# Chunk 5's gates by seven products, one of the sums on a PSUM bank that ScalarE fills, and a new order of the steps

## The chip, the cores and the metric

The kernel runs on one core of one Trainium2 chip. The metric is the device time of one execution in microseconds. A program's time is the median of its runs; the three runs of the kernel before lie between 249.38 and 249.58 us.

## The reference

Eight batches of 576 positions with 8 heads of 64 go through a linear attention, and the 4608 resulting rows of 512 go through a multiplicative feed-forward block:

```
phi(x) = where(x > 0, x, exp(x) - 1) + 1
kv  = sum over s of phi(k)[s] v[s]          z = sum over s of phi(k)[s]
x   = (phi(q) kv) / (phi(q) z + 1e-6)       per batch and head, then heads side by side
out = (((x @ w1) * (x @ w2)) @ w3) @ w_out  x: 4608 x 512, w1 and w2: 512 x 1024,
                                            w3: 1024 x 1024, w_out: 1024 x 512
```

Inputs and output are float32; the kernel's matmuls take bfloat16 and sum in float32.

## The kernel before

The product wf = w3 @ w_out is formed once, so each row of x needs two matrix products, the gates a = x w1 and b = x w2 with their elementwise product ab, and then out = ab wf. The rows are handled in 9 chunks of 512. Chunk c below 8 holds 512 of the 576 positions of batch c; chunk 8 holds the eight remainders of 64.

The program is a list of named steps, the string `ORDER`, carried out from left to right. `step` turns each name into a few instructions. The list alone sets in which order the instructions stand on each engine; the engines then run freely, each its own queue in order, and wait for one another by semaphores. The DMAs queue in the same way on SP and on POOL, and a DMA that waits holds back all that stand behind it on its queue. A `+` behind a step picks another engine for it: DVE in place of ScalarE for a copy, POOL in place of SP for a load. The steps that matter here:

- `L`, `M`, `N` load k, q and v of a batch in halves (512 KB each) into `ld` tiles, `R` the remainder of 64 positions (64 KB pieces, two for v, four for q and k).
- `x`, `y`, `z` (`X`, `Y`, `Z` for q) make phi of a half by ScalarE's exp (L179) and DVE's max and min (L184, L209); `v` casts v.
- `K` forms kv in a PSUM tile (L245), `T` transposes phi(q) by a DMA on SP into `qt` (L269), `A` multiplies the two and divides (L310, L326). `D` transposes the result `xn` by a DMA on SP into `xt` (L351), the moving operand of the gates; `D1.1`, `D3.1`, `D5.1`, `D7.1` do it for chunk 8 into `xtr`.
- `Fc.f` forms 128 columns of both gates of chunk c directly: eight matmuls with 512 moving columns into two banks `a_ps` and `b_ps` (L362), a ScalarE copy of one (L367), a DVE product with the other into `ab` (L368).
- `Gc.q.i` is used for chunks 6, 7 and 8 in place of `F`. It is Strassen's scheme with seven products for a 2 x 2 split of the weights' columns and the rows: product i of column pair q (columns q and q + 4) takes four matmuls with 256 moving columns (L422). It needs sums of weight blocks (steps `e`, kept in `ld` tiles named `spare`) and of xt blocks (steps `d`, L407). The products are summed in PSUM where they can be, in a bank `gu` (of the pool that the output also uses) and in banks `gt` of the pool `mm_ps`, which has four; where a bank is needed in two sums, ScalarE copies it into a half of a ring of `spare` tiles (L450) and DVE adds the copy to another bank (L454). Steps `m` then multiply the two gates, both in SBUF (L465), into `ab`; product 7 ends in a ScalarE copy of half a bank (L458) and a DVE product (L459).
- `Oc.m` is the output product of 128 rows of ab with wf: eight matmuls with 512 columns (L536), and a copy (L538). `S` and `H` store.

In the seven-product form a column pair has four quarters of ab to fill. Before, the quarter of products 1 and 2 is made as the others are: product 1 goes into `gu` and is copied to SBUF, product 2 goes into a bank of its own, DVE adds the two, DVE multiplies.

Of the kernel before, what the change touches and what calls it, by code (L numbers as in the profile page):

```python
# [20 lines left out]
def kernel(  # L21
# [388 lines left out]
    def g_product(t, c, q, a, m, first):  # L410

        for w in range(2):
            for k in range(2):
# [8 lines left out]
                nc.tensor.matmul(t[:, w], l, r, start=(first and w == 0 and k == 0), stop=(k == 1),  # L422
                                 skip_group_check=True)

    ring = []

    def fsm(name):
        if not spare.get("ring"):
            spare["ring"] = True
            for n in range(6):  # L430
                t = from_ld(("f", n), [P, 2, 2, HN], F32)
                ring.extend((t[:, 0], t[:, 1]))
        return ring.pop(0)

    def g_unit(c, q, i):
# [12 lines left out]
        if i in (1, 3, 4):  # L448
            s = st["s", i] = fsm("gs")
            nc.scalar.copy(out=s, in_=t)  # L450
        elif i in (2, 5, 6):
            s = st["c", i] = fsm("gc")
            o = st["s", {2: 1, 5: 4, 6: 3}[i]]
            nc.vector.tensor_tensor(out=s, in0=o, in1=t, op=ALU.add)  # L454
            ring.append(o)
        else:
            s = fsm("ga")
            nc.scalar.copy(out=s[:, 0], in_=t[:, 0])  # L458
            nc.vector.tensor_mul(out=abs_[c][:, q + 4, 0:HN], in0=s[:, 0], in1=t[:, 1])  # L459
            ring.append(s)  # L460

    def g_mul(c, q, i, alt):
        s = cs_[c, q]["c", i]
# [1 line left out]
        (nc.gpsimd if alt else nc.vector).tensor_mul(  # L465
            out=abs_[c][:, f, r * HN:(r + 1) * HN], in0=s[:, 0], in1=s[:, 1])
# [119 lines left out]
    A1.4 x2.1 F1.7 F1.6 x2.2 L2.0 y2.1 y2.2 Y2.0 x3.2 R3.1+ X2.0 O0.3 N2.1 x2.0 z2.1 N2.0 y2.0 z2.2  # L586
    Z2.0 F1.0 M3.0 R5.0+ y3.2 T2.0 v2.1 L3.0 Y3.1 R2.1+ F1.5 N3.1 v2.0+ z2.0 L3.1 Z3.1 v2.2+ O0.2
    F1.2 F1.1 Y3.0 y5.2 z3.2 K2 F1.4 A2.2 X3.0 F1.3 A2.3 x3.0 O0.1 Z3.0 A2.0 x3.1 N3.0 y3.0 O0.0
    v3.1 S0.1 A2.1 y3.1 R5.1+ z3.0 z3.1 v3.0 v3.2 O1.1+ O1.0 T3.0 D2.0 S0.0 L4.0 K3 R4.1+ R4.0+ O1.3
    A3.0 O1.2 A3.2 L4.1 v4.2+ F2.6 A3.3 F2.3 N4.1 y4.0 F2.1 M4.0 x4.0 A3.1 x4.1 F2.0 M4.1 y4.2 v5.2+  # L590
    x4.2 F2.7 Y4.0 D3.0 F2.4 z4.0 F2.2 X4.1 Y4.1 S1.0 F2.5 v4.1 Z4.1 N4.0 M5.0 X4.0 Z4.0 A3.4 z4.2
    y4.1 O2.3 F3.7 z4.1 M5.1 v4.0 A2.4 Y5.0 F3.6 L5.0 T4.0 M6.1 R6.0+ x5.2 Y5.1 X5.0 F3.1 N5.1 Z5.0
    S1.1 O2.2+ K4 F3.2 M6.0 x6.2 X5.1 A4.2 Z5.1 F3.4 z5.2 F3.5 y5.0 A4.1 F3.0 L5.1 F3.3 N5.0 y5.1
    X6.1 y6.2 O2.1 A4.3 R6.1+ N6.0 S2.1 x5.1 N6.1 v5.0+ T5.0 O2.0 x5.0 v5.1+ A4.0 R7.0+ z5.1 D4.0
# [5 lines left out]
    d6.0 v7.1 A6.4 e1.3 O5.1 O5.0 G6.1.1 G6.1.2 d6.1 G6.0.1 K7 d6.2 d6.3 G6.0.2 G6.0.3 m6.1.2 G6.0.4  # L600
    m6.0.2 S5.0 A7.3 G6.1.3 G6.0.5 G6.1.4 G6.1.5 m6.0.5 G6.2.4 G6.0.6 G6.0.7 G6.1.7 A7.0 G6.1.6
    G6.2.1 S4.0 G6.3.1 D5.1 G6.2.2 G6.2.3 G6.3.2 G6.3.3 m6.1.6 G6.2.5 G6.3.4 m6.2.2 G6.3.5 G6.2.6
    G6.2.7 A7.4 D7.1 G6.3.7 G6.3.6 O5.2 m6.3.5 A7.2 d8.0 O5.3 d8.2 G8.0.1 G8.0.4 m6.2.6 d8.1 m6.0.6
    d8.3 A7.1 G8.1.1 m6.3.6 G8.0.3 G8.0.2 G8.1.3 m6.2.5 G8.1.4 G8.0.5 G8.1.5 G8.3.4 G8.1.6 m8.0.2
    G8.0.7 G8.1.7 G8.2.4 m6.1.5 D7.0 G8.1.2 m8.0.5 d7.0 G8.2.1 S5.1 G8.3.1 G8.0.6 G8.2.3 m8.0.6
    G8.2.6 G8.3.3 G8.2.5 m6.3.2 G7.0.4 G8.3.5 G7.1.4 m8.1.2 G8.2.7 d7.1 G8.2.2 G8.3.7 d7.2 m8.1.5
    G8.3.6 O6.0 m8.3.5 m8.1.6 d7.3 O6.3 m8.2.5 O6.2+ m8.3.6 m8.2.6 O6.1 G7.0.1 m8.2.2 G8.3.2 G7.1.1
    m8.3.2 G7.0.3 S6.0 G7.0.6 G7.1.3 G7.0.5 G7.0.2 G7.1.5 G7.3.4 m7.1.5 G7.0.7 G7.2.4 m7.0.6 G7.1.7
    G7.1.6 m7.0.2 G7.2.1 G7.2.2 G7.3.1 S6.1 m7.2.2 G7.2.3 G7.2.6 G7.3.3 G7.2.5 G7.3.6 G7.3.5 G7.2.7
    G7.3.2 G7.1.2 G7.3.7 m7.3.2 m7.3.6 m7.1.2 O8.2 m7.3.5 O8.3 m7.0.5 O7.0 m7.2.6 O7.1 H8.2 m7.2.5  # L610
# [119 lines left out]
```

## Time and profile before

| | before |
|---|---|
| median of three runs | 249.55 us (249.38 to 249.58) |
| span of the profiled execution, first to last instruction | 248.0 us |
| own time of the profiled execution | not listed; its span stands 1.5 us below the median |
| TensorE (PE) busy | 230.9 us, 93% |
| VectorE (DVE) busy | 187.4 us, 76% |
| ScalarE (ACT) busy | 131.9 us, 53% |
| GpSimd (POOL) busy | 49.4 us, 20% |
| granted TensorE clock, mean | 0.991 |

The page divides the span into busy time by engine, and its groups by line give the mean duration of one instruction. PEld is the load of a matmul's stationary operand, which runs beside matmuls. Matmuls are pipelined: a group's mean of 379 ns is the time of one from its start to its modelled end, while the next one starts sooner, so the pace is read from the chain of waits, where runs of matmuls on one line are merged.

### The profile page before, as it was taken

To read this page: it belongs to the slowest core of one execution; us is meant where nothing else is said; L and a number is where in the kernel's file an instruction comes from. 1 tells how busy PE (TensorE), PEld (TensorE's weight loads), DVE (VectorE), ACT (ScalarE), POOL (GpSimd) and SP (SyncE) were. 2 spreads that over 40 slices of the span, in tenths; PEclk is the share of its full clock that TensorE was granted. 3 is DMA by queue.
4 is the path that set the end of the run, shared out by engine and by line. 5 is a ranking of instruction groups with operands and counts; after the bars stand their busy time and mean duration, and the time that the engine had idled before them with its cause. 6 is when DMAs were issued, how large, how long until landed. Compare 5 with 4: busy or idle time off the path is not lost.

```text
span 248.0 us, 4281 instructions
## 1 busy us (share of the span) xinstructions
PE 230.9 (93%) x1548; PEld 133.6 (54%) x1548; DVE 187.4 (76%) x434; ACT 131.9 (53%) x213; POOL 49.4 (20%) x79
## 2 busy tenths in 40 slices
PE   0699868999999999999999999999999999999994
PEld 0445455654454554345445544545488688578542
DVE  3227769777898847788768799988899999779810
ACT  2206667658756725675563383536466377245321
POOL 8546368665014050500000000000000000000000
...
GB/s 159 193 202 310 295 211 211 194 259 288 287 219 329 236 234 273 217 304 282 288 362 268 284 270 221 295 37 174 169 193 0 22 65 107 3 169 1 44 152 145
DMA packets 64021, 49.43 MB, mean 199 GB/s; under 512 B 32480, under 2 KB 58848, under 8 KB 64000
## 3 DMA queue, kind: packets, MB, share of 16 engines
...
q8 instruction: 12, 0.20, 0.3%
q10 hardware_dynamic: 144, 0.13, 0.2%
...
## 4 chain that ended last, share of the span: by engine, by line
PE 67%; DMA 21%; ACT 3%; DVE 3%; SPq 2%; issue 2%; POOL 0%; ACTq 0%; DVEq 0%; POOLq 0%
PE o_ps L536 21%; PE a_ps L362 12%; PE b_ps L362 12%; DMA q<-in_q_dram 10%; PE gu L422 9%; DMA w3b<-in_moe_w_dram 7%; PE gt L422 6%; DMA k<-in_k_dram 4%; PE nd L310 3%; PE kvp L245 2%; SPq L104 1%; ACT e L179 1%; PE o_ps L561 1%; PE kvp L249 1%; DVE qj L209 1%
## 5 line engine op out<-in xcount | busy, mean ns | idle before, releaser
L536 PE MATMUL o_ps<-wf_sb,ab 128*128 128x512 bf16 x280 | 64.2, 379 | 0.0
L362 PEld LDWEIGHTS <-w_sb 128*128 128x128 bf16 x384 | 36.5, 98 | 40.6 <-issue 0.8
L362 PE MATMUL a_ps<-xt,w_sb 128*128 128x512 bf16 x192 | 50.3, 379 | 0.5 <-ACT a_sb L367 0.5
L362 PE MATMUL b_ps<-xt,w_sb 128*128 128x512 bf16 x192 | 50.3, 379 | 0.0
L536 PEld LDWEIGHTS <-ab 128*128 128x128 bf16 x280 | 26.8, 98 | 29.3
L368 DVE TENSOR_TENSOR ab<-a_sb,b_ps 128x512 bf16<-128x512 f32 x48 | 32.5, 683 | 11.5 <-PE b_ps L362 5.9
L538 ACT COPY o_sb<-o_ps 128x512 f32<-128x512 f32 x30 | 17.4, 585 | 42.8 <-PE o_ps L536 28.8
L367 ACT COPY a_sb<-a_ps 128x512 f32<-128x512 f32 x48 | 27.7, 585 | 22.2 <-PE a_ps L362 21.8
L326 DVE TENSOR_TENSOR xn<-nd,r 128x512 bf16<-128x512 f32 x30 | 20.7, 691 | 1.0
L422 PEld LDWEIGHTS <-spare 128*128 128x128 bf16 x192 | 18.7, 98 | 2.2
L179 ACT ACTIVATE e<-q 128x1024 bf16<-128x1024 f32 x16 | 16.8, 1057 | 5.7 <-DMA q<-in_q_dram 5.0
L310 PE MATMUL nd<-kv,qt 128*128 128x130 bf16 (+1 forms) x160 | 16.6, 228 | 2.9 <-ACT kv L254 1.8
L179 ACT ACTIVATE e<-k 128x1024 bf16<-128x1024 f32 x16 | 16.8, 1056 | 3.2 <-DMA k<-in_k_dram 3.1
L310 PEld LDWEIGHTS <-qt 128*128 128x128 bf16 (+1 forms) x160 | 11.8, 103 | 12.2 <-issue 3.5
L454 DVE TENSOR_TENSOR spare<-spare,gt 128x512 f32<-128x512 f32 x24 | 16.1, 680 | 1.8 <-PE gt L422 0.9
L154 PE MATMUL wf_ps<-wt_sb,w3t 128*128 128x512 bf16 x64 | 16.5, 403 | 0.6 <-DMA wt_sb<-in_moe_w_out_dram 0.6
L450 ACT COPY spare<-gu 128x512 f32<-128x512 f32 x24 | 13.6, 587 | 3.9 <-PE gu L422 3.7
L422 PEld LDWEIGHTS <-w_sb 128*128 128x128 bf16 x144 | 14.0, 98 | 2.7 <-issue 0.3
L465 DVE TENSOR_TENSOR ab<-spare 128x256 bf16<-128x256 f32 x36 | 14.1, 417 | 0.1
L114 POOL DMA_DIRECT2D qk32r<-in_q_dram x14 | 9.0, 644 | 23.3 <-ACT a_sb L367 10.7
L209 DVE TENSOR_TENSOR qj<-e,y 128x512 bf16<-128x512 bf16 x32 | 12.1, 418 | 2.0 <-ACT e L179 1.8
L422 PE MATMUL gu<-spare 128*128 128x256 bf16 x96 | 13.4, 272 | 0.0
...
## 6 DMA issues: line engine op xcount, KB each, us to landing
out_dram<-o_sb SPq DMA_DIRECT2D x15, 512.0 KB, 3.9
q<-in_q_dram SPq DMA_DIRECT2D x13, 512.0 KB, 8.1
k<-in_k_dram SPq DMA_DIRECT2D x12, 512.0 KB, 7.0
v<-in_v_dram SPq DMA_DIRECT2D x12, 512.0 KB, 9.0
...
k<-in_k_dram POOLq DMA_DIRECT2D x4, 512.0 KB, 9.1
...
q<-in_q_dram POOLq DMA_DIRECT2D x3, 512.0 KB, 12.6
```

Of the source, the lines that this page charges most:

```text
L154: nc.tensor.matmul(wfs[i], w3ts[i][:, kc, :], wo_sb[:, kc, :], start=(kc == 0), stop=(kc == FC - 1))
L179: nc.scalar.activation(out=e, in_=x, func=AF.Exp)
L209: nc.vector.tensor_tensor(out=p[0][:, 2 * g + c].rearrange("p j u d -> p u j d"), in0=e[:, c], in1=y[:, c], op=ALU.min)
L310: nc.tensor.matmul(nds[g][rows, i * 2 * E1:(i + 1) * 2 * E1], w, kvs[b % 2][:, i, g].rearrange("p u e -> p (u e)"), start=True, stop=True)
L326: nc.vector.tensor_tensor(out=dst.rearrange("p (g h) e -> p g h e", g=2), in0=v4[:, :, :, 0:D], in1=r[rows].unsqueeze(3).to_broadcast([n, ...
L362: nc.tensor.matmul(ps, w[:, kc, f * P:(f + 1) * P], xt_of(c)[:, :, kc, :], start=(kc == 0), stop=(kc == KC - 1))
L367: nc.scalar.copy(out=a_sb, in_=a_ps)
L368: nc.vector.tensor_mul(out=abs_[c][:, f, :], in0=a_sb, in1=b_ps)
L422: nc.tensor.matmul(t[:, w], l, r, start=(first and w == 0 and k == 0), stop=(k == 1), skip_group_check=True)
L454: nc.vector.tensor_tensor(out=s, in0=o, in1=t, op=ALU.add)
L536: nc.tensor.matmul(o_ps, ab[:, f, m * P:(m + 1) * P], wf_sb[:, f, :], start=(f == 0), stop=(f == FC - 1))
L538: copy_of(alt)(out=rows_of(c, m // 2)[:, m % 2], in_=o_ps)
```

## The change

Chunk 5's gates are formed by the seven products too, so that `G` and `m` steps stand in the place of its eight `F` steps. For all four chunks in this form, the quarter of products 1 and 2 is made in another way: ScalarE copies product 1 from its bank `gu` into a bank `gt` instead of into SBUF, product 2 is accumulated onto that bank, and the quarter ends as that of product 7 does, with a ScalarE copy of half the bank and a DVE product of it with the other half. Four `m` steps with i = 2 per chunk and the DVE add of product 2 fall away. The weight sums of w1 now live in `wt_sb`, which held w_out for the prelude, not in `ld` tiles; the ring has 4 tiles in place of 6, and the small operands of products 2 and 7 lie in tiles of the pool `sm`. Of the list of steps the first 165 are as before; the rest is in another order, and some steps have another `+` (eight remainder DMAs move from POOL to SP).

```
     def ws_make(w, i, alt):
         t, s = (w1_sb, w2_sb)[w], wss[w]
-        s[i] = from_ld(("w", w, i // 2), [P, 2, 2, NQ * P], BF16)[:, i % 2]
+        if w == 0:
+            s[i] = wt_sb[:, i].rearrange("p a n -> p (a n)").rearrange("p (k n) -> p k n", k=2)
+        else:
+            s[i] = from_ld(("w", w, i // 2), [P, 2, 2, NQ * P], BF16)[:, i % 2]
...
+    NR = 4
...
-            for n in range(6):
+            for n in range(NR):
...
-        a, m, name, first = ((), ((0, 0, 0), (0, 0, 0), "u", True), ((0, 0, 1), (0, 1, 0), "t", True),
+        a, m, name, first = ((), ((0, 0, 0), (0, 0, 0), "u", True), ((0, 0, 1), (0, 1, 0), "t", False),
...
-        if i in (1, 3, 4):
+        if i == 1:
+            st["t"] = mm_ps.tile([P, 2, HN], F32, tag="mm", name="gt")
+            nc.scalar.copy(out=st["t"], in_=t)
+        elif i in (3, 4):
             s = st["s", i] = fsm("gs")
             nc.scalar.copy(out=s, in_=t)
-        elif i in (2, 5, 6):
+        elif i in (5, 6):
             s = st["c", i] = fsm("gc")
-            o = st["s", {2: 1, 5: 4, 6: 3}[i]]
+            o = st["s", {5: 4, 6: 3}[i]]
             nc.vector.tensor_tensor(out=s, in0=o, in1=t, op=ALU.add)
             ring.append(o)
         else:
-            s = fsm("ga")
-            nc.scalar.copy(out=s[:, 0], in_=t[:, 0])
-            nc.vector.tensor_mul(out=abs_[c][:, q + 4, 0:HN], in0=s[:, 0], in1=t[:, 1])
-            ring.append(s)
+            s = sm.tile([P, NCH], F32, tag="f", name="a_sb", bufs=4)[:, 0:HN]
+            nc.scalar.copy(out=s, in_=t[:, 0])
+            nc.vector.tensor_mul(out=abs_[c][:, q if i == 2 else q + 4, 0:HN], in0=s, in1=t[:, 1])
...
-        f, r = {2: (q, 0), 5: (q + 4, 1), 6: (q, 1)}[i]
+        f, r = {5: (q + 4, 1), 6: (q, 1)}[i]
...
     ORDER, a line of chunk 5 before and one after:
-    F4.1 S3.0 F4.4 D5.0 A5.4 y6.0 z6.0 F4.3 M7.1 F5.7 x7.2 y7.0 Y7.0 z7.2 L7.1 N7.0 K6+ z7.0 F5.6
+    N6.0 v6.0 D5.0 d5.2 d5.0 d5.1 N6.1 G5.0.1 R6.1 Z6.0 G5.1.1 F4.0 d5.3 G5.1.3 A4.4 G5.1.4 G5.0.3
```

On ScalarE's queue, at the start of chunk 7's gates, which both kernels form last: `o_ps` rows are the end of the output steps ahead of it, `gu` and `gt` are the banks of the products, `spare` is the ring in SBUF. Before:

```order
L538 COPY o_sb<-o_ps 128x512 x3
L450 COPY spare<-gu 128x512 x4
L450 COPY spare<-gt_2820 128x512
L458 COPY spare<-gu 128x256
L450 COPY spare<-gt_2833 128x512
L458 COPY spare<-gu 128x256
```

And now:

```order
L544 COPY o_sb<-o_ps 128x512 x3
L454 COPY gt<-gu 128x512
L457 COPY spare<-gt_2880 128x512
L454 COPY gt<-gu 128x512
L457 COPY spare<-gu 128x512 x2
L457 COPY spare<-gt_2915 128x512
L465 COPY a_sb<-gt 128x256
L465 COPY a_sb<-gu 128x256
```

The copy of product 1 goes into a bank now, and a second copy of half a bank (`a_sb<-gt`) has come in beside that of product 7.

On SP's queue, from the transpose of chunk 5's rows (`xt<-xn`) to the transpose of batch 6's phi(q) (`qt<-qj`). Before:

```order
L351 DMA_TRANSPOSE xt<-xn 128x16x128
L104 DMA q_1969<-in_q_dram 128x4x256
L104 DMA k_1993<-in_k_dram 128x4x256
L104 DMA v_1995<-in_v_dram 128x4x256
L546 DMA out_dram<-o_sb 128x1024
L269 DMA_TRANSPOSE qt<-qj 128x18x128 x2
```

And now:

```order
L351 DMA_TRANSPOSE xt<-xn 128x16x128
L104 DMA v_1937<-in_v_dram 128x4x256
L114 DMA v32r<-in_v_dram 64x4x64 x2
L104 DMA q_2017<-in_q_dram 128x4x256
L114 DMA qk32r<-in_q_dram 64x4x64 x2
L114 DMA qk32r<-in_k_dram 64x4x64 x2
L269 DMA_TRANSPOSE qt<-qj 128x18x128
```

Four DMAs stood between the two transposes, and eight stand there now, six of them the remainders that POOL issued before.

More of the change, by code (lines that the diff above doesn't have):

```diff
@@ L585 @@
     M2.1 M3.1 A1.3 F0.3 P1.3 X2.1 R2.0+ A1.0 L2.1 h0 h1 Y2.1 P1.0 M2.0 h2 h3 Z2.1 i0 i1 X3.1 R3.0+
[L586 to L594, printed above, removed]
@@ L600 @@
[L600 to L610, printed above, removed]
@@ L611 @@
-    H8.3 O8.0 m7.1.6 S7.0 O8.1+ S8.0 O7.2 H7.2 Q7.3
+    A1.4 x2.1 F1.7 F1.6 x2.2 N2.0 L2.0 M3.0 R3.1+ y2.2 O0.1 z2.2 R2.1+ v2.2+ Y2.0 Y3.1 X2.0 Z2.0
+    F1.1 N2.1 Z3.1 y2.0 F1.0 x2.0 z2.0 y2.1 z2.1 O0.3 L3.0 v2.0 v2.1 T2.0 y3.2 F1.3 x3.2 Y3.0 F1.4
+    L3.1 X3.0 Z3.0 K2 O0.0 y3.0 z3.2 x3.1 A2.2 F1.2 y3.1 N3.1 v3.1 A2.0 e0.2 x3.0 F1.5 N3.0 v3.0
+    S0.0 O0.2 A2.3 O1.3 z3.0 v3.2 A2.1 L4.1 x4.1 T3.0 R6.0+ R5.0+ z3.1 D2.0 S0.1 O1.2+ K3 O1.0 e1.2
+    A3.3 e1.0 L4.0 O1.1 A3.1 F2.6 A3.2 M4.0 F2.4 F2.1 y4.1 A3.0 F2.0 e1.1 F2.2 A3.4 S1.1 D3.0 R4.0+
@@ new lines @@
+    x4.2 y4.2 z4.2 X4.0 M5.1 M4.1 F2.5 z4.1 y4.0 x5.2 F2.7 S1.0 y5.2 Y4.0 z5.2 F2.3 x4.0 Z4.0 F3.4
+    F3.3 Y5.1 N4.1 z4.0 M5.0 Y4.1 R4.1+ v4.2 R5.1+ O2.0+ X4.1 Z4.1 N4.0 A2.4 F3.0 N5.1 v4.0+ F3.2
+    X5.0 v4.1+ T4.0 e0.0 Y5.0 F3.1 X5.1 Z5.1 v5.1 Z5.0 O2.1 K4 O2.2 A4.1 O2.3 L5.1 y5.1 A4.0 L5.0
+    y5.0 M6.1 y6.2 F3.5 x5.1 z5.1 S2.0 A4.2 Y6.1 X6.1 N5.0 F3.7 F3.6 x5.0 z5.0 S2.1 T5.0 A4.3 D4.0
+    v5.0 Z6.1 v5.2+ e0.1 O3.3 O3.0 K5 O3.1 e1.3 A5.3 M6.0 O3.2 e0.3 A5.0 D3.1 F4.5 A5.1 Y6.0 x6.2
+    z6.2 F4.2 F4.6 S3.0 A5.2 X6.0 L6.1 y6.1 x6.1 z6.1 F4.7 F4.3 A5.4 L6.0 x6.0 F4.4 y6.0 z6.0 F4.1
@@ new lines @@
+    A6.4 G6.0.3 G6.0.4 G6.1.5 G6.1.2 G6.0.5 m5.2.6 m6.0.5 K7 S5.0 G6.0.7 G6.0.6 G6.1.6 G6.1.7 G6.2.1
+    T7.0 A7.1 G6.2.4 G6.0.2 G6.2.3 G6.2.6 G6.3.1 G6.2.5 A7.4 G6.2.2 G6.3.3 G6.2.7 D7.1 G6.3.2 m5.0.5
+    G6.3.4 G6.3.5 A7.3 O5.2+ G6.3.7 G6.3.6 D1.1 d8.0 d8.1 m6.1.6 m6.2.5 m6.1.5 d8.2 A7.2 G8.0.1
+    m6.2.6 O5.3 G8.0.4 G8.0.3 m6.3.6 G8.1.1 G8.3.4 G8.0.6 d8.3 G8.0.5 G8.1.3 G8.0.2 G8.1.4 G8.1.5
+    G8.0.7 S5.1 G8.1.6 G8.1.2 G8.1.7 G8.2.1 G8.2.4 m8.0.6 m8.0.5 A7.0 G8.3.1 m8.1.6 G8.2.3 G8.2.6
+    G8.3.3 G8.2.5 G8.2.2 G8.3.5 G8.3.2 G8.2.7 G8.3.6 G8.3.7 S4.0 O8.0+ O8.1+ m6.0.6 D7.0 d7.0 O6.0
@@ L612 @@
+    S8.0 d7.1 m6.3.5 O6.3+ O6.2 O6.1 d7.2 G7.0.1 d7.3 G7.0.4 G7.1.1 m8.2.6 G7.0.3 G7.0.6 m8.1.5
+    G7.1.3 G7.0.5 G7.1.4 G7.1.5 G7.0.2 G7.0.7 G7.2.4 m8.3.6 m7.0.5 G7.1.7 G7.1.2 m7.1.5 G7.2.1
+    G7.1.6 m7.1.6 G7.3.1 G7.2.3 G7.2.6 G7.3.3 G7.2.5 m7.2.5 S6.1 G7.3.2 G7.3.4 G7.3.5 G7.2.7 G7.2.2
+    G7.3.6 G7.3.7 S6.0 O7.0+ m7.3.5 O7.1 S7.0 m8.3.5 m7.3.6 m8.2.5 O8.2 H8.2 O8.3 H8.3 m7.0.6 m7.2.6
+    O7.2 H7.2 Q7.3
     """
```

9 lines of the change are left out of this document (5 added, 4 removed).

## The prediction

> **What bounds the kernel now.** First the page's head, the busy time by stage and the granted clock; in the rows by stage the columns are PE, PEld, DVE, ACT and POOL busy, then the clock, the DMA engines' share and GB/s.
>
> ```profile
> span 248.0 us, 4281 instructions
> PE 230.9 (93%) x1548; PEld 133.6 (54%) x1548; DVE 187.4 (76%) x434; ACT 131.9 (53%) x213; POOL 49.4 (20%) x79
> ...
> 45.00:125.00 80.00, 79.27 (x493) 40.17 (x491) 63.70 (x147) 49.06 (x77) 22.08 (x36) 1.00 1.12 265
> 125.00:175.00 50.00, 49.53 (x289) 24.68 (x288) 43.07 (x98) 26.07 (x39) 0.00 (x0) 1.00 0.93 232
> 175.00:243.00 68.00, 67.99 (x511) 47.97 (x510) 54.50 (x124) 33.69 (x65) 0.00 (x0) 1.00 0.29 85
> ```
>
> From 45 us to 243 us TensorE is busy for 196.8 of 198 us at the full clock. The 165 steps that stay as they are end in this stretch (at about 62 to 64 us), so what is reordered is all work of a saturated TensorE. The time of the reordered part is the sum of its matmuls plus TensorE's waits; another engine matters only where TensorE waits for it. DVE is second, with 54.5 of 68 us in the last stage.
>
> A busy row could hide a slow pace, so next the chain of waits (start, length, what), where merged runs give the true pace, and TensorE's waits (total us, times, longest):
>
> ```profile
> 60.36 0.86 PE b_ps L362 x4
> ...
> 91.59 12.85 DMA q<-in_q_dram
> ...
> 118.44 9.40 DMA k<-in_k_dram
> ...
> 185.55 0.44 PE gt L422 x4
> ```
>
> ```profile
> PE nd L310 <- DVE xn L326: 0.8, 2, 0.5
> PE a_ps L362 <- ACT a_sb L367: 0.5, 1, 0.5
> PE nd L310 <- DVE xnr L326: 0.2, 1, 0.2
> ```
>
> Four matmuls of 512 columns take 0.86 us, four of 256 columns 0.44 us: the pace goes with the columns in both forms, and the weight loads are hidden in both. The waits that lie in the reordered part come to about 1.5 us. The chain shows what stands behind them: a load of q that lands 12.85 us after its issue and one of k 9.40 us after, which held up ScalarE and DVE.
>
> **The change part by part.** *TensorE.* Chunk 5 loses eight `F` steps of eight matmuls: 64 x 0.86/4 = 13.76 us. It gains four column pairs of seven products of four matmuls: 28 x 0.44 = 12.3 us (12.2 at 0.436, half of the 0.87 that the chain gives for eight). All other matmuls keep number and shape. As TensorE is the bound, all of it is on the path: **-1.5 us**.
>
> *VectorE and ScalarE.* The groups (busy, mean ns of one):
>
> ```profile
> L362 PE MATMUL a_ps<-xt,w_sb 128*128 128x512 bf16 x192 | 50.3, 379 | 0.5 <-ACT a_sb L367 0.5
> L422 PE MATMUL gu<-spare 128*128 128x256 bf16 x96 | 13.4, 272 | 0.0
> L368 DVE TENSOR_TENSOR ab<-a_sb,b_ps 128x512 bf16<-128x512 f32 x48 | 32.5, 683 | 11.5 <-PE b_ps L362 5.9 <-ACT a_sb L367 5.1 <-PE tpr L277 0.2
> L367 ACT COPY a_sb<-a_ps 128x512 f32<-128x512 f32 x48 | 27.7, 585 | 22.2 <-PE a_ps L362 21.8
> L454 DVE TENSOR_TENSOR spare<-spare,gt 128x512 f32<-128x512 f32 x24 | 16.1, 680 | 1.8 <-PE gt L422 0.9 <-ACT spare L450 0.7
> L465 DVE TENSOR_TENSOR ab<-spare 128x256 bf16<-128x256 f32 x36 | 14.1, 417 | 0.1
> L450 ACT COPY spare<-gu 128x512 f32<-128x512 f32 x24 | 13.6, 587 | 3.9 <-PE gu L422 3.7
> L459 DVE TENSOR_TENSOR ab<-spare,gu 128x256 bf16<-128x256 f32 x12 | 4.9, 416 | 0.6 <-ACT spare L458 0.6
> L458 ACT COPY spare<-gu 128x256 f32<-128x256 f32 x12 | 4.5, 373 | 4.9 <-PE gu L422 4.2 <-DVE ab L459 0.5
> L407 DVE TENSOR_TENSOR spare<-xt 128x512 bf16<-128x512 bf16 x4 | 1.7, 419 | 0.6 <-DMA xt<-xn 0.6
> ```
>
> DVE per column pair, before: three adds, three SBUF products, one product from a bank, 3 x 0.68 + 3 x 0.417 + 0.416 = 3.71 us. Now two, two and two: 3.03 us. Chunk 5 adds 4 x 3.03 + 4 x 0.419 (its `d` steps) - 8 x 0.683 = +8.3 us; chunks 6 to 8 give back 12 x 0.68 = 8.2 us. DVE's total stays where it was, and in a stretch of products alone it asks 3.03 us for the 3.05 us that TensorE needs for a pair, not 3.71. The eight weight sums `e` are the same work at an earlier place, moved out of the stretch in which batches 6 and 7 and the first sums meet. Cost on the path: nothing; the cover is TensorE's own work.
>
> ScalarE per pair, before: 3 x 0.587 + 0.373 = 2.13 us. Now 3 x 0.587 + 2 x 0.373 = 2.51 us. Chunk 5: 4 x 2.51 - 8 x 0.585 = +5.4 us; the others 12 x 0.373 = +4.5 us; some casts moved from DVE about +1.4 us. 131.9 becomes about 143 us of 246. In the products 2.51 of 3.05 us: still no bound on average, but single copies are waited for.
>
> *The new wait.* How closely a copy is followed shows where chunk 7's gates begin (start, length, engine, what):
>
> ```profile
> 218.42 0.60 PE L422 MATMUL gu<-xt,w_sb 128*128 128x256 bf16 x4
> ...
> 219.10 0.59 ACT L450 COPY spare<-gu 128x512 f32<-128x512 f32 x1
> ...
> 219.29 0.60 PE L422 MATMUL gu<-xt,w_sb 128*128 128x256 bf16 x4
> ...
> 219.74 0.60 PE L422 MATMUL gu<-spare 128*128 128x256 bf16 x4
> 219.93 1.07 ACT L450 COPY spare<-gu 128x512 f32<-128x512 f32 x2 [0.24 <-PE gu L422]
> ```
>
> The product begun at 219.29 hands over at 219.29 + 0.44, and its copy starts at 219.93: 0.20 us. The copy at 219.10 ends at 219.69, and the product that adds to the same bank starts at 219.74: 0.05 us. So copy and hand-overs take 0.20 + 0.587 + 0.05 = 0.84 us, two products in between give 0.87 us of cover, and one copy queued ahead uncovers it. Product 3 had to wait for the copy of product 1 before too; that it now goes into a bank changes only the copy's length. Product 2 must newly wait for that copy, and behind it in TensorE's queue stands everything; but the list puts at least four products between the two, 4 x 0.436 = 1.7 us against the 0.84 us needed: free, unless ScalarE is 0.9 us behind. No row shows a ScalarE copy from bank to bank. From below I allow 0.48 us, what two copies in a row are apart in the last row (0.585 in all, less their overlap: 1.07 - 0.59); from above the 0.69 us of the slowest 128x512 operation of the groups, DVE's. I take 0.587, the same engine, source and size. At 0.69 the six closest places (two products of cover) would lose 6 x 0.1 = 0.6 us, at 0.48 nothing is won beyond small change. The Trainium skill (ScalarE: Activation LUTs, Step-by-step: what each stage is for) says that ScalarE reaches PSUM faster than SBUF, with the caveat that this helps only if TensorE doesn't need most of PSUM. By the first half the term is 0 or slightly below; the caveat speaks against this change, since a bank stays taken from the copy of product 1 to the product on DVE. No run here shows either yet.
>
> *Banks.* Before, a pair took two `mm_ps` banks for short times; now the first is held longer, through most of the pair. Two pairs in work hold two of four, and a direct gate step needs two: in chunk 5's first pair `F4.0` stands between the first products, and it just fits. I cost this at 0.1 us.
>
> *The order.* The stalls of about 1.5 us came from late loads, not from a shortage of an engine; in the new order other loads are close. I placed the loads of each half ahead of their first use by the list, with about 0.5 us of issue and 1.5 us per 512 KB, and find slack of 0 to 3 us, as before. I let 1.1 of the 1.5 us remain, by judgment: between 0 and twice what was. Term **-0.4**, ends -1.5 and +1.5. To it +0.1 for products that wait a few hundredths.
>
> **Sum.** -1.5 - 0.4 + 0.1 = -1.8 on the span, 246.2 us. The medians stand 1.5 us above the profiled span; 249.55 - 1.8 = **247.7 us**.
>
> **The rivals.** *Late transposes, slower than before.* On SP a DMA transpose waits out what is ahead of it:
>
> ```profile
> 152.67 0.50 SPq L546 DMA_DIRECT2D out_dram<-o_sb  x1
> 153.29 7.21 SPq L269 DMA_TRANSPOSE qt<-qj  x1
> ...
> qt<-qj SPq DMA_TRANSPOSE x6, 7.1
> ...
> v<-in_v_dram SPq DMA_DIRECT2D x12, 512.0 KB, 9.0
> ...
> v32r<-in_v_dram POOLq DMA_DIRECT2D x14, 64.0 KB, 6.5
> ...
> v32r<-in_v_dram SPq DMA_DIRECT2D x2, 64.0 KB, 7.5
> ...
> qk32r<-in_k_dram SPq DMA_DIRECT2D x2, 64.0 KB, 12.7
> ```
>
> Batch 6's transpose of phi(q) now stands behind eight DMAs, six of them remainders that POOL issued before. From the last `A5` on which chunk 5's transpose rests to `A6.1`, the first use, TensorE has 17.2 us of work. The chain needs about 1.3 us for DVE, 0.5 us for the first transpose, 8 x 0.5 = 4 us of issue, the landing of the last remainder, and some 2.5 us for the transpose itself (the 7.21 us above are mostly queue): 8.3 us plus the landing. With 7.5 us it just fits; with the 12.7 us of the other row TensorE waits (8.3 + 12.7) - 17.2 = 3.8 us, for 247.7 + 3.8 = 251.5 us. It decides from a landing of about 9 us on; from 10.8 us the gain is gone. For it: SP's own row. Against it: that row is from the start, when all queues were full, and a DMA share of 0.93 or less is met here. Chance 0.13. The Trainium skill (DMA: Bandwidth & Descriptors, Issuing engines are not separate DMA queues) says that all issuers share the same engines and that only issue time differs; by that the move would cost SP's 4 us of issue and no more, which fits into 17.2 us, and the rows of 6.5 and 7.5 us agree.
>
> *ScalarE or a bank becomes the bound in the products.* Every third closest place loses a copy's queue of 0.3 us, 16 pairs lose 0.1 us each: +1.6 us, 249.3 us, no change that can be told. For it: 2.51 of 3.05 us and 0.03 us of margin. Against it: two copies in a row start 0.48 us apart, so ScalarE catches up. Chance 0.12.
>
> *All stalls go.* Only the closer packing of matmuls remains: -1.5 - 1.5 = 246.5 us; it needs every load early. Chance 0.1.
>
> **How the numbers follow.** Forecast 0.65, at 247.7 us, its own range 246.8 to 248.8. A run of this kernel can tell 0.2% or 0.5 us from no change, so faster is below 249.05 and slower above 250.05. Faster: 0.65 + 0.1 = 0.75, less 0.01 for the forecast's edge, 0.74; same: 0.12; slower: 0.13 and that edge, 0.14. The range 246.4 to 249.7 leaves out the late transpose and little else.
>
> **What would show it.** TensorE's busy time about 1.5 us lower and still whole between 45 us and the end; DVE near 187 us, ScalarE near 143 us; no TensorE wait of over 0.3 us for the copy L454; products of L422 paced at 0.44 us per four. The forecast is wrong if TensorE waits for `qt`, if the waits of `nd` and `a_ps` grow beyond 2 us, or if product 3 waits for L454 at most places.

## The result, and the profile after

| | before | after |
|---|---|---|
| median, first measurement | 249.97 us (20 runs) | 248.59 us (20 runs) |
| ratio, 95% interval | | 0.995 (0.993 to 0.997) |
| the same two again, on another chip | 250.41 us (12 runs) | 248.09 us (7 runs) |
| ratio, 95% interval | | 0.9923 (0.9893 to 0.9952) |
| span of the profiled execution | 248.0 us | 246.7 us (time 248.52) |

The change makes the kernel faster, by 1.2 us in the first measurement and 1.9 us in the second (249.6 x 0.005 and x 0.0077). The medians alone differ by 1.4 and 2.3 us; the text goes by the ratios, which come with intervals. The forecast of 247.7 us against 249.55 was a ratio of 0.9926.

The page's head and the busy time by stage of the new kernel, columns as before:

```profile
span 246.7 us, 4411 instructions
PE 229.1 (93%) x1596; PEld 137.9 (56%) x1596; DVE 187.6 (76%) x439; ACT 141.2 (57%) x240; POOL 43.9 (18%) x71
...
45.00:125.00 80.00, 78.70 (x477) 39.67 (x476) 64.47 (x146) 48.47 (x78) 15.65 (x26) 1.00 1.04 261
125.00:175.00 50.00, 49.89 (x345) 30.05 (x344) 45.13 (x107) 34.53 (x58) 0.00 (x0) 1.00 0.91 230
175.00:243.00 68.00, 67.35 (x514) 48.27 (x512) 51.12 (x121) 34.78 (x72) 0.00 (x0) 1.00 0.36 90
```

TensorE is still busy nearly all the time from 45 us on, 195.9 of 198 us against 196.8. VectorE stands where it stood, ScalarE has 9.3 us more. TensorE's waits behind 45 us (total us, times, longest):

```profile
PE a_ps L362 <- ACT a_sb L367: 0.8, 1, 0.8
PE gu L425 <- DMA xtr<-xnr: 0.6, 1, 0.6
PE a_ps L362 <- DMA xt<-xn: 0.5, 1, 0.5
```

None of them is a wait of the new sum. They are three single places, here in TensorE's timeline (start, length, what, idle time ahead):

```profile
90.36 1.02 PE L362 MATMUL a_ps<-xt,w_sb 128*128 128x512 bf16 x4 [0.54 <-DMA xt<-xn]
...
94.97 1.02 PE L362 MATMUL a_ps<-xt,w_sb 128*128 128x512 bf16 x4 [0.77 <-ACT a_sb L367]
...
195.40 0.61 PE L425 MATMUL gu<-xtr,w_sb 128*128 128x256 bf16 x4 [0.61 <-DMA xtr<-xnr]
```

Matmuls overlap, so start to start these places lose a little more than the idle time: 0.70, 0.93 and 0.77 us, 2.4 us in all. What the gain consists of is seen when the same event is looked up in both traces. Batch 1's last small product lies in the part of the list that did not change; the last group of matmuls ends the kernel. Before, then after:

```profile
58.98 0.41 PE L310 MATMUL nd<-kv,qt 128*64 128x130 bf16 x4
...
242.60 1.91 PE L561 MATMUL o_ps<-wf_sb,ab 128*128 128x256 bf16 x16
```

```profile
58.06 0.41 PE L310 MATMUL nd<-kv,qt 128*64 128x130 bf16 x4
...
241.32 1.91 PE L567 MATMUL o_ps<-wf_sb,ab 128*128 128x256 bf16 x16
```

From the one to the other it is 183.62 us before and 183.26 us after: 0.36 us of the 1.28 us between the two profiled executions lie in the reordered part, and 0.92 us ahead of it, where the steps are the same. In the second profile of the new kernel the first event stands at 57.86 us, in two variants below at 59.01 and 59.50: this start drifts by 1.6 us between profiled executions whose steps are the same up to there. So one pair of profiles can't carry a verdict on 1 us; the medians do, and the profile tells the places. In the second profile of the new kernel the stretch between the two events takes 181.81 us (57.86 to 239.67), 1.45 us less than in the first, for the same list.

### The profile page after: what moved, and what is told of

Its sections match the earlier page's. It is cut to its first block, busy times and chain, and to the rows that moved or that the text cites. A ratio compares the mean times of both kernels' runs of the same rounds, so it can differ in the third digit from the quotient of the medians.

```text
span 246.7 us, 4411 instructions
## 1 busy us (share of the span) xinstructions
PE 229.1 (93%) x1596; PEld 137.9 (56%) x1596; DVE 187.6 (76%) x439; ACT 141.2 (57%) x240; POOL 43.9 (18%) x71
## 4 chain that ended last, share of the span: by engine, by line
PE 67%; DMA 19%; DVE 6%; ACT 3%; issue 2%; POOL 1%; SPq 0%; DVEq 0%; ACTq 0%; POOLq 0%
PE o_ps L542 20%; PE a_ps L362 14%; PE b_ps L362 13%; PE gu L425 8%; PE gt L425 6%; DMA k<-in_k_dram 5%; DMA q<-in_q_dram 5%; DMA wt_sb<-in_moe_w_out_dram 3%; DMA v32r<-in_v_dram 3%; PE nd L310 3%; DMA xt<-xn 2%; DVE spare L461 2%; PE kvp L245 1%; DMA xtr<-xnr 1%; ACT spare L457 1%
## 5 line engine op out<-in xcount | busy, mean ns | idle before, releaser
L362 PE MATMUL a_ps<-xt,w_sb 128*128 128x512 bf16 x160 | 42.7, 384 | 1.3 <-ACT a_sb L367 0.8
L362 PE MATMUL b_ps<-xt,w_sb 128*128 128x512 bf16 x160 | 42.0, 379 | 0.0
L368 DVE TENSOR_TENSOR ab<-a_sb,b_ps 128x512 bf16<-128x512 f32 x40 | 26.9, 683 | 11.1 <-ACT a_sb L367 6.5
L367 ACT COPY a_sb<-a_ps 128x512 f32<-128x512 f32 x40 | 23.1, 587 | 19.4 <-PE a_ps L362 19.2
L461 DVE TENSOR_TENSOR spare<-spare,gt 128x512 f32<-128x512 f32 x16 | 10.8, 682 | 4.8 <-ACT spare L457 4.2
L425 PEld LDWEIGHTS <-wt_sb 128*128 128x128 bf16 x128 | 12.1, 98 | 2.7
L425 PEld LDWEIGHTS <-spare 128*128 128x128 bf16 x128 | 12.5, 98 | 1.5
L114 POOL DMA_DIRECT2D qk32r<-in_q_dram x12 | 7.5, 626 | 32.4 <-DVE o_sb L544 30.3
L147 PE MATMUL w3p<-ident,w3b 128*128 128x128 bf16 x64 | 6.3, 265 | 7.2 <-DMA w3b<-in_moe_w_dram 7.2
L209 DVE TENSOR_TENSOR kj<-e,y 128x512 bf16<-128x512 bf16 x32 | 12.1, 419 | 0.8 <-ACT e L179 0.7
```

Source lines behind the costliest of these rows:

```text
L209: nc.vector.tensor_tensor(out=p[0][:, 2 * g + c].rearrange("p j u d -> p u j d"), in0=e[:, c], in1=y[:, c], op=ALU.min)
L362: nc.tensor.matmul(ps, w[:, kc, f * P:(f + 1) * P], xt_of(c)[:, :, kc, :], start=(kc == 0), stop=(kc == KC - 1))
L367: nc.scalar.copy(out=a_sb, in_=a_ps)
L368: nc.vector.tensor_mul(out=abs_[c][:, f, :], in0=a_sb, in1=b_ps)
```

## The experiments

Ratios are to the kernel before on the same chip, with their 95% intervals. "Behind the new kernel" takes the new kernel's first ratio, 0.995; against its second, 0.9923, such a distance is 0.7 us larger. The experiments fall into three groups: which part of the change does what, how much room the new sum leaves, and where the three stalls come from.

**1. Chunk 5 direct again, the rest as in the new kernel.** Its 28 products, `d` and `m` steps go, eight `F` steps come, evenly spread:

```
-    N6.0 v6.0 D5.0 d5.2 d5.0 d5.1 N6.1 G5.0.1 R6.1 Z6.0 G5.1.1 F4.0 d5.3 G5.1.3 A4.4 G5.1.4 G5.0.3
+    N6.0 v6.0 D5.0 N6.1 R6.1 Z6.0 F5.0 F4.0 A4.4 F5.1
```

> The new kernel with chunk 5's gates formed directly again: eight F steps stand in the place of its 28 products, evenly spread, and its d and m steps fall away; everything else of the new list stays. Theory, the gain is the matmuls: 64 matmuls of 0.216 us come back for 112 of 0.109 us, 13.8 - 12.2 = +1.6 us against the new kernel, so a ratio of about 1.001 to the kernel before (new kernel: 0.995), TensorE's busy time up by about 1.5 us and its stalls as in the new kernel. Rival, the gain comes from the new order: the time stays where the new kernel's is, ratio 0.995.

Measured: 250.33 us, 1.0025 (0.9998 to 1.0051), TensorE busy 231.5 us against 229.1. Against the new kernel's 0.995 that is +0.75%, 1.9 us, where the sum of the matmuls gave 1.6. The gain hangs on chunk 5's matmuls; new order and new sum without it are no faster than the kernel before. The stalls were not "as in the new kernel": start to start, the first place loses 0.88 us, the other two nothing, and one new wait for a copy 0.40 us. From batch 1's last small product to the last group this kernel takes 183.55 us, 0.3 us more than the first profile of the new kernel with its 2.4 us of stalls, and 1.7 us more than the second with 0.95 us (experiment 8).

**2. The new sum alone, in the order of before.** The g_unit of the change for chunks 6 to 8, `m` steps with i = 2 taken out, and product 2 behind three others (in two pairs two are left of them):

```
-    G6.1.1 G6.1.2 d6.1 G6.0.1 K7 d6.2 d6.3 G6.0.2 G6.0.3 m6.1.2 G6.0.4
+    G6.1.1 d6.1 G6.0.1 K7 d6.2 d6.3 G6.0.3 G6.1.2 G6.0.4 G6.0.2
```

> The kernel before, its own order, chunk 5 direct, with only the new sum in chunks 6 to 8: product 1 is copied by ScalarE into a bank, product 2 is accumulated there; product 2 of each pair is moved to behind three other products after product 1, and the m steps with i = 2 fall away. Theory, DVE is not on the path: VectorE 12 x (0.68 + 0.417 - 0.416) = 8.2 us less busy, about 179 us, ScalarE 12 x 0.373 = 4.5 us more, about 136 us, the time within 0.3 us of the kernel before (ratio 0.999 to 1.001). Rival 1, VectorE held TensorE up in the products: 0.5 us faster or more (ratio below 0.998). Rival 2, the bank that is held longer costs: 0.5 us slower or more.

Measured: 254.17 us, 1.0166 (1.0135 to 1.0197): rival 2. VectorE is at 181.0 us, where about 179 had been worked out, and it didn't help. One of TensorE's longest waits in the products, and the only one of a product 2, on TensorE and on ScalarE:

```profile
206.84 1.08 PE L422 MATMUL gu<-xtr,w_sb 128*128 128x256 bf16 x8
...
209.73 0.49 PE L422 MATMUL gt<-xtr,w_sb 128*128 128x256 bf16 x3 [0.51 <-ACT gt L450]
```

```profile
207.47 0.57 ACT L450 COPY gt<-gu 128x512 f32<-128x512 f32 x1
209.11 0.57 ACT L450 COPY gt<-gu 128x512 f32<-128x512 f32 x1 [1.07 <-DVE spare L457]
```

Two products 1 end at 207.72 us, one behind the other. The second one's copy could follow at 208.0 but begins at 209.11, since no bank is free for it to fill until a VectorE add (L457) has read one; product 2 stands at the head of TensorE's queue and waits, three products behind product 1 though it is. The sum takes work off VectorE, but it needs a bank from product 1 on, in the middle of a list that was laid out for one that needs it later (three of the 12 pairs had product 2 directly behind product 1). This place loses 0.67 us, start to start, of the 4 us by which the kernel is slower; in all, TensorE's waits in the products grow from 0.43 us in three places to 5.0 us in 17, for ScalarE's copies and for VectorE. What the 4 us are the price of stays open. The experiment also moved product 2: in six of the 12 pairs it stands nearer to product 1 than before, and in experiment 7 a product 2 as near as here costs as much in the new order. The old order with product 2 further back was not run.

**3. The old sum in the new order.** Product 1 is copied to SBUF, product 2 has its own bank, VectorE adds and multiplies:

```
-            st["t"] = mm_ps.tile([P, 2, HN], F32, tag="mm", name="gt")
-            nc.scalar.copy(out=st["t"], in_=t)
+            st["p"] = sm.tile([P, 2, HN], F32, tag="f", name="p1", bufs=6)
+            nc.scalar.copy(out=st["p"], in_=t)
+        elif i == 2:
+            nc.vector.tensor_tensor(out=st["p"], in0=st["p"], in1=t, op=ALU.add)
+            nc.vector.tensor_mul(out=abs_[c][:, q, 0:HN], in0=st["p"][:, 0], in1=st["p"][:, 1])
```

> The new kernel, its order and chunk 5 by seven products, with the old form of the sum: product 1 is copied to SBUF, product 2 goes to a bank of its own, VectorE adds and then multiplies in SBUF right behind. VectorE 16 x 0.68 = 10.9 us more busy, about 198 us, ScalarE 16 x 0.373 = 6 us less. Theory, the new sum is what lets four chunks of products pass: VectorE asks 3.71 us per pair against TensorE's 3.05, falls behind in the stretch from 175 us on, and TensorE waits 1 to 4 us for banks (249.6 to 252.6 us on the new kernel's scale of 248.6). Rival, the sum changes nothing that TensorE sees: within 0.3 us of the new kernel.

Measured: 256.94 us, 1.0269 (1.0228 to 1.031): 8 us behind the new kernel, in the theory's direction and twice its size. From 150 us to 210 us, in two stages:

```profile
150.00:176.00 26.00, 24.38 (x192) 17.02 (x190) 25.14 (x59) 18.11 (x31) 0.00 (x0) 1.00 0.83 218
176.00:210.00 34.00, 31.42 (x264) 23.73 (x263) 32.67 (x79) 16.57 (x33) 0.00 (x0) 1.00 0.42 94
...
PE gu L425 <- DVE spare L464: 3.2, 6, 0.9
PE o_ps L545 <- DVE ab L469: 1.3, 2, 0.8
```

VectorE is busy for 57.8 of 60 us there, and it is VectorE that TensorE waits for. The same two stages in the new kernel, and the second of them in the kernel before:

```profile
150.00:176.00 26.00, 25.89 (x201) 17.92 (x199) 25.17 (x61) 19.51 (x35) 0.00 (x0) 1.00 0.91 243
176.00:210.00 34.00, 33.35 (x295) 26.90 (x293) 31.43 (x77) 20.98 (x45) 0.00 (x0) 1.00 0.44 91
```

```profile
176.00:210.00 34.00, 34.00 (x293) 26.70 (x292) 32.17 (x76) 20.74 (x40) 0.00 (x0) 1.00 0.34 90
```

VectorE has 3.4 of 60 us left in the new kernel, with nothing added. The average of 76% hid this; I had put the four added chunk-5 pairs beside TensorE's work by totals. But a high share alone is no stall: in the kernel before VectorE is busy for 32.17 of 34 us, and TensorE for all 34. How much of the 8 us is the added work and how much its place directly behind product 2 was not separated.

**4. The copies of half banks made twice.**

```
             nc.scalar.copy(out=s, in_=t[:, 0])
+            nc.scalar.copy(out=s, in_=t[:, 0])
             nc.vector.tensor_mul(out=abs_[c][:, q if i == 2 else q + 4, 0:HN], in0=s, in1=t[:, 1])
```

> The new kernel with the ScalarE copies of half banks (products 2 and 7) made twice into the same tile: 32 more of 0.373 us, 0.27 us apart when they follow each other, so ScalarE asks 3.05 to 3.26 us per pair in the products, where TensorE needs 3.05. Theory of the prediction, ScalarE is no bound and has about 0.5 us per pair to spare: TensorE's waits in the products, 0.9 us in all in the new kernel, grow by less than 1 us, total within 1 us of the new kernel. Rival, ScalarE or a bank it fills already stands at the bound in the products: every added copy shows, 32 x 0.27 = 8.6 us, or at least 3 us, slower.

Measured: 253.32 us, 1.0144 (1.011 to 1.0178), 4.8 us behind the new kernel for 10.2 us more of ScalarE (151.4 us). The 0.5 us per pair that ScalarE was to have to spare are not there: half of the added time shows.

**5. The added copies off the chain.** The second copy reads the SBUF tile and goes to another one, so that VectorE need not wait for it:

```
             nc.scalar.copy(out=s, in_=t[:, 0])
+            nc.scalar.copy(out=sm.tile([P, NCH], F32, tag="f", name="a2", bufs=4)[:, 0:HN], in_=s)
```

> The new kernel with a further ScalarE copy behind each half-bank copy, as in the kernel with these copies doubled, but from the SBUF tile into another SBUF tile that nobody reads: 32 more copies on ScalarE, and VectorE's product no longer waits for the second. Theory 1, the chain counts (copy, VectorE's product, the next add in VectorE's queue, the bank): ScalarE alone has room, within 1.5 us of the new kernel. Theory 2, ScalarE's time counts: as slow as the kernel with the copies doubled, 253.3 us, 4 to 5 us behind the new kernel.

Measured: 252.54 us, 1.0118 (1.0066 to 1.017), 4 us behind the new kernel: theory 2, ScalarE's time itself. One place, first on ScalarE, then on TensorE:

```profile
230.19 0.41 ACT L466 COPY a<-a_sb 128x256 f32<-128x256 f32 x1
230.50 0.36 ACT L465 COPY a_sb<-gt 128x256 f32<-128x256 f32 x1
230.90 0.41 ACT L466 COPY a<-a_sb 128x256 f32<-128x256 f32 x1
231.21 1.06 ACT L454 COPY gt<-gu 128x512 f32<-128x512 f32 x2
```

```profile
231.84 0.38 PE L425 MATMUL gu<-spare,wt_sb 128*128 128x256 bf16 x2 [0.58 <-ACT gt L454]
```

The two copies nobody reads (L466) push the copy of product 1 back, and product 3 waits 0.58 us. With ScalarE busy for 60% of the span, every microsecond added in the products costs 0.4 us (4.2 us for 10.4).

**6. Product 2 directly behind product 1**, in all 16 pairs of the new kernel:

```
-    G6.3.1 G6.2.5 A7.4 G6.2.2 G6.3.3 G6.2.7 D7.1 G6.3.2
+    G6.3.1 G6.3.2 G6.2.5 A7.4 G6.3.3 G6.2.7 D7.1
```

> The new kernel with product 2 of all 16 pairs moved to directly behind product 1. By the prediction's chain (hand-over 0.20, copy 0.587 or the 0.577 that the copy into a bank now shows, hand-over 0.05) TensorE waits 0.83 us at each of them: 16 x 0.83 = 13.3 us, about 262 us where the new kernel has 248.6, a little less where other waits of the products are swallowed (10 us at least). Rival, the copy is not what product 2 waits for, or banks that come free sooner pay it back: less than 5 us.

Measured: 266.63 us, 1.0677 (1.0635 to 1.072). The waits, and the first two of them:

```profile
PE gt L425 <- ACT gt L454: 11.1, 16, 0.8
...
152.83 0.60 PE L425 MATMUL gu<-xt,w_sb 128*128 128x256 bf16 x4
154.09 0.60 PE L425 MATMUL gt<-xt,w_sb 128*128 128x256 bf16 x4 [0.66 <-ACT gt L454]
```

The second begins 154.09 - 152.83 = 1.26 us after product 1, 0.82 us later than its own 0.44 us allow, and most of the others lose the same. The chain of 0.84 us was right. The whole costs 18 us, 5 us more than expected. In the profile the 16 places lose 13.7 us, start to start, and TensorE's other waits behind 59 us grow from 3.3 to 6.2 us (the one for `D1.1` alone from 0.77 to 1.45): what stands behind is late in its turn.

**7. Product 2 behind two others.**

```
-    G6.3.1 G6.2.5 A7.4 G6.2.2 G6.3.3 G6.2.7 D7.1 G6.3.2
+    G6.3.1 G6.2.5 A7.4 G6.3.3 G6.3.2 G6.2.7 D7.1
```

> The new kernel with product 2 of all 16 pairs moved to behind two other products after product 1: 2 x 0.436 = 0.87 us of cover against a chain of 0.83 us. Theory, the cover is all that counts: at most 0.1 us per pair, within 1.5 us of the new kernel. Rival, a copy stands behind other copies in ScalarE's queue (0.27 to 0.48 us for each) at many places, so that two products don't cover it and the 4 to 14 of the new list are needed: 16 x 0.2 to 0.4 = 3 to 6 us slower.

Measured: 252.44 us, 1.0107 (1.0071 to 1.0143), 4 us behind the new kernel, the size that the rival gave. But product 2 loses 0.13 us in one place and nothing in the other 15, so the cover is as worked out; other products wait:

```profile
PE gu L425 <- DVE spare L461: 0.8, 3, 0.3
...
PE gu L425 <- ACT spare L457: 0.7, 3, 0.2
```

So neither expectation holds as it was argued: the wait is not where the rival had it. Moving 16 products by a few places made others wait for copies and sums; why just these was not followed further. The list has little room at these places.

**8. The new kernel again,** as a yardstick for the three beside it.

> The new kernel unchanged, on the same chip as the three kernels beside it, as their yardstick: ratio to the kernel before between 0.993 and 0.997, as in the first measurement. Both theories of where its stalls come from expect the same three in its trace: about 0.7 us before chunk 2's first direct gate step, up to 0.9 us at a copy of a chunk 2 gate, about 0.8 us before chunk 8's first product.

Measured: 248.09 us, 0.9923 (0.9893 to 0.9952), just below the expected 0.993 to 0.997. The three places are there, but smaller: the a_ps after `D2.0` 0.21 us late, the copy 0.34, chunk 8's first product 0.41 (start to start), 0.95 us in place of 2.4:

```profile
93.69 1.02 PE L362 MATMUL a_ps<-xt,w_sb 128*128 128x512 bf16 x4 [0.17 <-ACT a_sb L367]
...
193.76 0.61 PE L425 MATMUL gu<-xtr,w_sb 128*128 128x256 bf16 x4 [0.24 <-DVE ab L466]
```

**9. D1.1 early.**

```
-    G5.3.6 m5.3.6 G6.1.1 G6.0.1 D5.1 G6.1.4 G6.1.3
+    G5.3.6 m5.3.6 G6.1.1 G6.0.1 D5.1 D1.1 G6.1.4 G6.1.3
-    G6.3.4 G6.3.5 A7.3 O5.2+ G6.3.7 G6.3.6 D1.1 d8.0 d8.1
+    G6.3.4 G6.3.5 A7.3 O5.2+ G6.3.7 G6.3.6 d8.0 d8.1
```

> The new kernel with one step moved: D1.1, the transpose of the remainders of batches 0 and 1, stands right behind D5.1 in place of behind D7.1, some 15 us earlier on SP. Theory, TensorE's 0.77 us at the first product of chunk 8 is that transpose, landing 0.6 us behind D7.1: the wait goes and the time falls by 0.6 to 0.8 us, 0.997 of the new kernel; the next step that needs D7.1 itself (the sum d8.0, and then the fourth product) comes 2 us later and is in time. Rival, the product waits for D7.1 in any case: 0.1 us are won, no change that can be told.

Measured: 247.73 us, 0.99 (0.9869 to 0.993); chunk 8's first product waits for nothing:

```profile
194.96 0.60 PE L425 MATMUL gu<-xtr,w_sb 128*128 128x256 bf16 x4
```

The stall was D1.1. The gain, 0.23% against the kernel of 8, is smaller than the intervals; the timeline shows that the stall is gone, the times alone don't show a gain. The other two places lose 1.15 us in this profile, 0.54 us in that of 8.

**10. The remainder loads away from D2.0.** On POOL batch 4's remainders go first, those of batches 6 and 5 are released by D2.0:

```
-    A2.1 L4.1 x4.1 T3.0 R6.0+ R5.0+ z3.1 D2.0 S0.1 O1.2+
+    A2.1 L4.1 x4.1 T3.0 R4.0+ z3.1 D2.0 R6.0+ R5.0+ S0.1 O1.2+
-    GATES = "R6.0<T3.0 M2.1<B0.0"
+    GATES = "R6.0<D2.0 M2.1<B0.0"
```

> The new kernel with the remainder loads of q and k on POOL in another order: batch 4's first and not gated, batches 6 and 5 released only when D2.0, the transpose of chunk 2's rows, has landed (before: when the transpose T3.0 ahead of it had). Theory, the sixteen small loads that start at the same time as D2.0 hold it up, 6.06 us to landing against 4.3 us for the others of its kind: D2.0 lands 1 us or more earlier, TensorE's stall of 0.70 us before chunk 2's first gate step goes, 0.5 to 0.7 us faster than the new kernel (0.9975). Rival, D2.0 is late for its place on SP and what DVE hands it: it lands where it did, and the stall stays at 0.6 to 0.9 us.

Measured: 248.02 us, 0.9909 (0.9886 to 0.9932). How long that transpose took to land, in the new kernel and here:

```profile
L351 SPq DMA_TRANSPOSE xt<-xn x1: 2674/2674/2674, 84.3 to 84.3; - x1
...
DMA to landing us min/median/max: 6.1/6.1/6.1
```

```profile
L351 SPq DMA_TRANSPOSE xt<-xn x1: 2847/2847/2847, 85.1 to 85.1; - x1
...
DMA to landing us min/median/max: 4.2/4.2/4.2
```

In kernels 8 and 9, whose POOL list is the new kernel's, it took 5.6 and 6.1 us, and in all nine profiled kernels with that list 5.6 to 6.3 us; in the three with this edit (10, 11 and 12) it took 4.2 to 4.4 us. (Eight of the small loads had been issued when it landed; "sixteen" in the expectation counts all that follow.) TensorE's stall before chunk 2 is gone, and the one at the copy is gone with it. That one's cause is on ScalarE, in the new kernel and here:

```profile
93.35 1.07 ACT L544 COPY o_sb<-o_ps 128x512 f32<-128x512 f32 x2 [6.64 <-PE a_ps L362]
94.31 1.09 ACT L367 COPY a_sb<-a_ps 128x512 f32<-128x512 f32 x2
```

```profile
91.95 1.07 ACT L544 COPY o_sb<-o_ps 128x512 f32<-128x512 f32 x2 [4.38 <-DMA out_dram<-o_sb]
92.91 1.22 ACT L367 COPY a_sb<-a_ps 128x512 f32<-128x512 f32 x2
```

The page names TensorE in the first, but its releaser had long been done: the copy needs the tile that a store behind D2.0 on SP still reads, issued at 87.02 us and landed 6.2 us later, at 93.25. Here that store lands after 3.8 us. Both stalls had one cause, the small loads that start with the transpose.

The time can't tell this kernel from that of 8, and the stretch between the two events takes 181.77 us, as in the profile of 8 (181.81): the third stall, which this edit leaves, loses 0.96 us here and 0.41 us there. It is the wait for `D1.1` again; this transpose landed at 194.74 us, and the view names a VectorE step done before:

```profile
194.79 0.61 PE L425 MATMUL gu<-xtr,w_sb 128*128 128x256 bf16 x4 [0.80 <-DVE spare L461]
```

**11. All three.** The edits of 9 and 10, and three tiles for the output in place of two:

```
-            o_sbs[c, r] = sm.tile([P, 2, DM], F32, tag="o_sb", name="o_sb", bufs=2)
+            o_sbs[c, r] = sm.tile([P, 2, DM], F32, tag="o_sb", name="o_sb", bufs=3)
```

> The new kernel with both of these moves and a third output tile o_sb (three buffers for two), so that a ScalarE copy need not wait for the store of two tiles before. Theory, the three stalls are independent and TensorE is the bound everywhere else: -0.7 - 0.77 and 0.3 to 0.9 us for the copy, 1.5 to 2.4 us faster than the new kernel, 0.985 to 0.989 of the kernel before, TensorE's stalls behind 45 us at 2.3 to 3.2 us against 4.7. Rival, what goes at one place comes back at the next (the late chain of loads keeps its rhythm): less than 0.7 us faster.

Measured: 247.20 us, 0.987 (0.984 to 0.99), the fastest kernel of all. No wait of TensorE behind 45 us is left in that view, and from batch 1's last small product, at 59.53 us, to the last group it is 180.80 us, where the kernel before takes 183.62:

```profile
59.53 0.41 PE L310 MATMUL nd<-kv,qt 128*64 128x130 bf16 x4
...
240.33 1.91 PE L567 MATMUL o_ps<-wf_sb,ab 128*128 128x256 bf16 x16
```

That is 0.9 us less than the kernel of 8 on the same chip, below the theory's 1.5 to 2.4 because the stalls there were 0.95 us and not 2.4. The two intervals overlap, so the times make it likely and no more; that the three stalls are gone is shown. Since the copy's stall went without it in 10, the third tile has shown no worth.

**12. Three swaps on top,** each a product 7 of which TensorE still waited 0.2 to 0.3 us for a VectorE add:

```
-    G5.2.6 G5.2.7 m5.0.6 Y7.0 X7.0 L7.1 x7.1 L7.0 m5.2.5 Z7.0 G5.2.2
+    G5.2.6 G5.2.2 m5.0.6 Y7.0 X7.0 L7.1 x7.1 L7.0 m5.2.5 Z7.0 G5.2.7
-    G6.0.7 G6.0.6 G6.1.6
+    G6.0.6 G6.0.7 G6.1.6
-    G8.3.6 G8.3.7
+    G8.3.7 G8.3.6
```

> The kernel with the three stalls taken out (remainders gated on D2.0, D1.1 early, three output tiles), and three swaps of neighbouring products where the new kernel's TensorE still waited 0.27, 0.16 and 0.21 us for VectorE: product 7 of pair 2 of chunk 5 with product 2, product 7 of pair 0 of chunk 6 with its product 6, product 7 of pair 3 of chunk 8 with its product 6. Theory: these 0.64 us go, 0.984 to 0.987 of the kernel before, about 1 to 2.5 us faster than the new kernel. Rival, product 6 or 2 then waits in place of product 7, or the DVE adds behind it: no faster than without the swaps, 0.987.

Measured: 248.94 us, 0.9961 (0.9929 to 0.9993): the rival, and worse. On TensorE, then on VectorE:

```profile
172.65 0.59 PE L542 MATMUL o_ps<-wf_sb,ab 128*128 128x512 bf16 x2 [2.06 <-DVE ab L466]
```

```profile
170.57 0.68 DVE L184 TENSOR_SCALAR y<-q 128x1024 bf16<-128x1024 f32 x1
171.18 0.42 DVE L471 TENSOR_TENSOR ab<-spare 128x256 bf16<-128x256 f32 x1
171.51 0.75 DVE L209 TENSOR_TENSOR qj<-e,y 128x512 bf16<-128x512 bf16 x2
172.18 0.41 DVE L466 TENSOR_TENSOR ab<-a_sb,gu 128x256 bf16<-128x256 f32 x1
```

The swap put product 7's VectorE product (172.18 us) behind batch 7's phi steps in VectorE's queue; its bank came free 2 us later, and the output step that needs the bank waited. A wait of 0.27 us had become one of 2.06.

## Why the prediction was right, point by point

- *TensorE, -1.5 us: right.* Undoing just this term cost 1.9 us (experiment 1), at intervals of some 0.8 us.
- *Stalls from late loads, -0.4 us: the term that failed in sign in the profiled execution.* It began from a misreading: of the 1.5 us of waits, 0.35 us lie at 39.15 us, in the part that did not change. Start to start, TensorE lost 1.60 us at three places of the reordered part before (0.68, 0.29 and 0.63), and loses 2.40 us in the first profile of the new kernel and 0.95 us in the second: +0.8 and -0.65 us in place of -0.4. Slack by "0.5 us of issue and 1.5 us per 512 KB" left out that a transpose on SP takes longer beside the small loads that POOL starts at the same moment (4.2 us became 6.1), and that `D1.1` now stood behind `D7.1`. The ends of -1.5 and +1.5 held both draws; how near the forecast came hung on which one was drawn, and that was luck.
- *The terms together:* 112 x 0.109 - 64 x 0.216 = -1.62 us of matmuls, the stalls and the small waits (+0.5, next point) make -0.3 us for the first profile and -1.8 for the second; between the two events it is 183.26 - 183.62 = -0.36 and 181.81 - 183.62 = -1.81 us. So the profiles leave no larger term out. Whether the two ratios, 0.995 and 0.9923, differ for the same reason was not shown.
- *Small waits of the products, +0.1 us: too small.* Start to start, TensorE lost 0.44 us in three places of the 12 pairs before (0.145, 0.17, 0.12) and loses 0.92 us in seven places of the 16 pairs now, the largest 0.27: +0.5 us.
- *VectorE and ScalarE totals: right,* 187.6 us for 187 and 141.2 for about 143. *What I made of them was not.* "VectorE asks 3.03 us for 3.05" leaves no margin, and from 150 to 210 us VectorE is busy for 56.6 of 60 us (experiment 3). "ScalarE catches up" holds for this list alone (experiments 4 and 5).
- *The new wait: right.* Product 2 waits nowhere in the new kernel, and where it is made to wait, the chain is 0.82 us for 0.84 (experiment 6). The copy from bank to bank lies between my bounds:

```profile
L457 ACT COPY spare<-gu 128x512 f32<-128x512 f32 x16 | 9.5, 591 | 2.7 <-PE gu L425 2.1 <-DVE ab L471 0.3
L454 ACT COPY gt<-gu 128x512 f32<-128x512 f32 x16 | 9.1, 577 | 3.7 <-PE gu L425 3.4
```

  The Trainium skill (ScalarE: Activation LUTs, Step-by-step: what each stage is for) has ScalarE reach PSUM faster than SBUF; this trace agrees in sign, 577 to 591 ns, a difference that decides nothing here. Its caveat on PSUM is nearer to what matters: in experiment 2 a copy waited 1.07 us for a bank to fill.
- *Late transposes, the slower rival: no.* The transpose of batch 6's phi(q) was issued at 153.83 us, landed 4.6 us later at 158.47, and TensorE first uses it at 161.01. From chunk 5's transpose to this one SP took 8.7 us (145.18 to 153.83), where the sum had 0.5 + 4 us of issue. What kept it in time were the six remainders ahead of it, which landed in 4 to 5 us, well below the 9 us from which the rival decides:

```profile
v32r<-in_v_dram SPq DMA_DIRECT2D x2, 64.0 KB, 4.4
qk32r<-in_q_dram SPq DMA_DIRECT2D x2, 64.0 KB, 5.1
qk32r<-in_k_dram SPq DMA_DIRECT2D x2, 64.0 KB, 4.1
```

  The Trainium skill (DMA: Bandwidth & Descriptors, Issuing engines are not separate DMA queues) says that all issuers share the same engines. Experiment 10 agrees from the other side: with the small loads that POOL issued beside it, a transpose issued by SP took 6.1 us in place of 4.2.
- *ScalarE or a bank as the bound: not in this kernel, but it has little room:* 10 us more work for ScalarE costs 4 us (experiment 5).
- *"All stalls go", 246.5 us, 0.1:* experiment 11 is that case, made by hand; its 0.987 is 246.3 us on the scale of 249.55.
